# Mixing's first batch in another order: channel weights decoded first, the first group's angles while tokens still load, several token sums at once in separate banks

## The chip, the cores and the metric

The kernel runs on one core of a Trainium2 chip. The metric is device time in microseconds (us). Five engines work beside each other, each through its own instructions in order: PE (matrix products), DVE and ACT (vector work, ACT also sine and absolute value), POOL (more vector work and the indirect transfers), and SP, which here only issues DMA transfers. PE writes into PSUM, which this kernel divides into banks of 128 x 512 float32; SBUF holds everything else.

## The reference

Three stages follow each other; the change is in the third alone.

```python
scores = where(q @ k.T * scale >= max - tau, ..., -1e9); x = softmax(scores) @ v     # attention
out[b, s] = p[e] * (relu(x[b, s] @ w1[e]) @ w2[e])          # one of 8 experts per token
theta = x @ w_theta                                         # mixing, x: (4, 576, 512)
zr, zi = x * cos(theta), x * sin(theta)
y = einsum('ts,bsd->btd', w_tok_r, zr) + einsum('ts,bsd->btd', w_tok_i, zi)
u = x + y
return u + maximum(u @ w_ch, 0)
```

## The kernel before

Attention runs to about 300 us, the routed experts to about 616 us, mixing from there to the end. Every matrix product is made of three: operands are split into a high and a low part (names ending in h and l), and high x high, high x low and low x high are summed in PSUM.

**Weights.** The weights come as 64-bit words. To decode one block of 128 x 512 (`decode_chunk`) takes four DVE instructions (L1109, L1113, L1116, L1118), one square on POOL (L1110), then a copy on ACT and a subtraction on POOL (L1101, L1102, both in `split_last`) that make the high and the low part. `decode(n)` writes n such DVE steps into the order, with two blocks in flight; `decode_rest` writes what is left. The channel weights `ch` are four such blocks, of 0.5 MB of words each (L1075).

**A batch of mixing.** The 576 tokens of a batch are five chunks: four of 128, and one of 64, which two batches share. `prep` transposes a chunk (L1290, PE), takes the high part (xTh, ACT, L1291) and the low part (xTl, DVE, L1292), and copies the sum to xTf (ACT, L1296; the last 64 columns by POOL at L1280). `theta(b, dh, g)` makes the angles of half dh of the channels (256 each) for group g of the chunks (0: chunks 0 and 1; 1: chunks 2 and 3; 2: the fifth), 24 products (L1311 to L1313), 12 for group 2. `wave_steps` takes them on, step by step: k on ACT (L1330), four DVE steps that bring the angle into range (L1332, L1334, L1336, L1338), absolute value, sine and cosine on ACT (L1339 to L1341), two products with x on DVE (L1344, L1346; for the fifth chunk four small ones, L1353), and the split of the results: zrh, zih, zmh on ACT (L1360), zrl, zil, zml on POOL (L1361). A string such as `self.wave("0011")` says which group advances next: each digit is one step of that group.

`mix(b, dh, g)` then sums 27 products (L1374 to L1376) over all z of half dh into one bank, for one quarter g of its outputs: four such sums per half. `mix_out` adds x (u, DVE, L1387) and after two quarters splits u (uu: ACT L1389, DVE L1390). `channel` multiplies u with the channel weights (L1400 to L1402), adds (DVE, L1404), and `store` transposes and writes out.

**Order.** PE, ACT and DVE run their instructions in the order in which the code writes them (`MANUAL`); POOL and the DMA queue of SP are put in order by a scheduler. In batch 0, `prep` handles all five chunks first, then all angles of both halves are multiplied, then the waves run, then the sums `mix`, one bank at a time from a pool of two (`ps_y`). The channel weights are decoded between the sums of batch 0, one block at a time (`decode(4)`). Batch b+1 is prepared between the sums of the second half of batch b.

```python
            self.mix(b, 1, 0)
            self.mix_out(b, 1, 0)
            if more:
                self.prep(b + 1, (0, 1), (0, 1))
```

Of the kernel before, what the change touches and what calls it, by code (L numbers as in the profile page):

```python
# [15 lines left out]
ALU = mybir.AluOpType  # L16
# [19 lines left out]
RING, HIDDEN_STEPS, LAST_STEPS, PRE_STEPS = 3, 4, 5, 9  # L36
# [15 lines left out]
class Kernel:  # L52
# [1080 lines left out]
    def mixing(self):  # L1133
        nc, tc = self.nc, self.tc
        with ExitStack() as ctx:
            def pool(name, bufs, **kw):
                return ctx.enter_context(tc.tile_pool(name=name, bufs=bufs, **kw))
            self.ch = pool("chp", 1).tile([P, 2, 4, DM], F32R, name="ch")
            self.zp, self.xp3, self.tmp = pool("zp", 2), pool("xp3", 1), pool("tmp", 2)
# [3 lines left out]
            self.state3 = [{} for _ in range(B)]  # L1143
            self.work = []
            with tc.manual_schedule(engines=MANUAL):
                self.mix_all(ctx)

    def mix_all(self, ctx):
# [13 lines left out]
        self.prep(0, (3,), (1,))  # L1162
        self.decode(3)
        self.theta(0, 0, 0)
        self.prep(0, (4,), (2,))
        for dh in range(2):
            for g in range(1 - dh, 3):
                self.theta(0, dh, g, self.ps_v if dh or g == 2 else self.ps_th)
        self.waves(0, 0)
        self.wave("0d1")  # L1170
        self.prep(0, (), (3, 4))
        self.wave("0d0d0d0" "21d1d1d1" "00" "0" "2d2d2d2" "11" "1" "22" "2")
# [3 lines left out]
        self.open_stage(1, 2)  # L1176
        self.todo = self.square_words("moe2_w_ch", self.ch)
        self.stage_words()
        self.waves(0, 1)
        self.wave("012" "01010101" "2222")  # L1180
        self.rest = []
        for b in range(B):
            more = b + 1 < B
            self.mix(b, 0, 0)
            while self.rest:
                self.rest.pop(0)()
            self.mix_out(b, 0, 0)
            self.wave("0011" "0")
            self.mix(b, 0, 1)
            self.mix_out(b, 0, 1)  # L1190
            if b == 0:
                self.decode(4)
            self.wave("1")
            self.mix(b, 0, 2)
            self.mix_out(b, 0, 2)
            self.wave("222")
            self.mix(b, 0, 3)
            self.mix_out(b, 0, 3)
            if b == 0:
                self.decode(4)  # L1200
            if more:
                self.load_x(b + 1)
            self.mix(b, 1, 0)
# [3 lines left out]
            self.mix(b, 1, 1)  # L1207
            self.mix_out(b, 1, 1)
            if more:
                chunks = (2, 3) if b % 2 == 0 else (2, 3, 4)  # L1210
                self.prep(b + 1, chunks, chunks)
                if b == 0:
                    self.decode(4)
# [6 lines left out]
            if b == 0:  # L1220
                self.decode_rest()
                self.stage.close()
                self.op = self.right.enter_context(self.tc.tile_pool(name="op", bufs=4, side="right"))
# [23 lines left out]

    def waves(self, b, dh):
        self.work = [self.wave_steps(b, dh, g) for g in range(3)]
# [9 lines left out]
    def load_x(self, b):  # L1259
# [3 lines left out]
        if b % 2:  # L1263
            for n in ("x", "xh", "xl"):
                st[n] = self.state3[b - 1][n]
        else:
            st["x"] = self.xp3.tile([P, NC, DM], F32, name="xm")
        x, m = st["x"], self.m_dram[b * S:]
        for c, e in ((0, 2), (2, 4)) if b else ((0, 1), (1, 2), (2, 4)):
            nc.sync.dma_start(x[:, c:e, :], m[c * P:e * P, :].rearrange("(c p) d -> p c d", p=P))  # L1270
        if b % 2 == 0:
            for t in range(2):
                nc.sync.dma_start(x[t * D:(t + 1) * D, 4, :], m[t * S + 4 * P:(t + 1) * S, :])
            st["xh"] = self.xp3.tile([P, 4, NC * P], F32R, name="xTh")
            st["xl"] = self.xp3.tile([P, 4, NC * P], F32R, name="xTl")
# [6 lines left out]
    def prep(self, b, chunks, rest=()):  # L1282
# [3 lines left out]
        for c in chunks:  # L1286
# [5 lines left out]
            nc.vector.tensor_tensor(st["xl"][:, :, cs], t, st["xh"][:, :, cs].bitcast(F32), ALU.subtract)  # L1292
# [199 lines left out]
```

## Time and profile before

| what | us |
|---|---|
| three runs | 878.38, 882.13, 882.84 (median 882.13) |
| profiled execution | 878.96 |
| its span | 877.1 |
| PE busy in the span | 819.7 (93%) |
| DVE, ACT, POOL busy | 608.8, 480.4, 267.1 |

The profiled execution is 878.96 us by the same clock as the runs; its span, from the first to the last instruction in the trace, is 877.1 us, so 1.9 us lie around it. All times in the trace count from the start of the span. Matrix instructions overlap each other, so their durations are longer than their distance. Idle time before an instruction is printed in square brackets with what ended it.

### The profile page before, as it was taken

The page shows a single profiled execution, that of the slowest core. Times are in us where ns is not written, and L with a number is a line of the kernel's source. Part 1 is how long each engine was busy: PE and PEld are TensorE (multiplying, and loading weights), DVE is VectorE, ACT ScalarE, POOL GpSimd, SP SyncE. Part 2 cuts the span into 40 slices and gives each one's busy share as a digit, 9 for nine tenths or more (in the row PEclk, how much of TensorE's full clock was granted, in tenths as well). Part 3 has the DMA queues.
Part 4 walks back from the last instruction along what each step waited for, and adds up shares of the span by engine and source line. Part 5 has one row for each costly group of instructions (what it writes and reads, how often), then busy time and mean ns, then how long its engine had stood idle before and what let it go on. Part 6 is the DMA issues. An engine that isn't in the chain of part 4 may idle for free.

```text
span 877.1 us, 15357 instructions
## 1 busy us (share of the span) xinstructions
PE 819.7 (93%) x5608; PEld 659.2 (75%) x5608; DVE 608.8 (69%) x1245; ACT 480.4 (55%) x803; POOL 267.1 (30%) x289
## 2 busy tenths in 40 slices
PE   7999998999899995899999999989788999999997
PEld 4565555656556653688999889966688999999997
DVE  6888786887679948539888888545198854745432
ACT  5777675766576654536555556455364533536311
POOL 4222124224114205216445554111125530331220
PEclk9999999999899999999999999999999999999999
DMA  6423213312321269248877787764203020030101
GB/s 164 103 58 99 57 58 92 86 56 69 97 68 59 57 239 235 84 145 275 298 239 257 260 265 240 247 251 138 70 1 96 25 93 23 1 102 1 37 19 54
DMA packets 64903, 105.67 MB, mean 120 GB/s; under 512 B 28338, under 2 KB 32566, under 8 KB 64824
## 3 DMA queue, kind: packets, MB, share of 16 engines
q1 hardware_dynamic: 60632, 94.15, 34.9%
q0 software_dynamic: 4192, 10.51, 3.5%
q8 instruction: 45, 0.74, 0.4%
q14 instruction: 34, 0.28, 0.1%
HBM read 98.67 MB, written 15.40 MB: 130 GB/s over the span
## 4 chain that ended last, share of the span: by engine, by line
PE 32%; DVE 8%; issue 5%; DMA 5%; ACT 2%; POOL 1%; SPq 0%; DVEq 0%; POOLq 0%; ACTq 0%
PE y L1376 3%; PE y L1374 3%; PE y L1375 3%; PE o L951 2%; PE v L1401 2%; PE o L952 2%; PE o L950 2%; PE v L1402 2%; PE v L1400 2%; PE h L935 2%; PE h L934 2%; PE h L933 2%; DMA scr_m<-raw,idx 1%; PE th L1313 1%; PE th L1312 1%
## 5 line engine op out<-in xcount | busy, mean ns | idle before, releaser
L314 ACT ACTIVATE e<-ns,nb 128x576 f32<-128x576 f32 x144 | 111.8, 777 | 59.1 <-DVE ns L308 57.9
L308 DVE TENSOR_SCALAR_CACHE_REDUCE ns<-s,nqs 128x576 f32<-128x576 f32 x144 | 116.7, 811 | 26.0 <-PE s L288 15.9
L346 DVE SCALAR_TENSOR_TENSOR a<-ns,thr,e 128x576 f32<-128x576 f32 x144 | 117.0, 813 | 11.9 <-POOL thr L321 8.3
L321 POOL TENSOR_SCALAR thr<-nb,tauoff 128x2 f32<-128x2 f32 (+1 forms) x80 | 57.0, 713 | 170.3 <-DVE ns L308 170.1
L288 PE MATMUL s<-raw 64*128 64x288 f32 x512 | 87.5, 442 | 15.0 <-DVE ns L308 14.5
L361 ACT ACTIVATE aT<-t 128x512 f32<-128x512 f32 x128 | 70.4, 594 | 28.4 <-PE t L360 27.3
L401 PE MATMUL o<-aT,vm 128*64 128x288 f32 x512 | 78.2, 427 | 0.0
L288 PEld LDWEIGHTS s<-raw 64*128 64x128 f32 x512 | 42.4, 186 | 43.1 <-DVE ns L308 21.2
L933 PE MATMUL h<-xh,stk 128*128 128x256 f32 x256 | 73.3, 286 | 0.0
L1031 DVE TENSOR_TENSOR w2l<-w2r,w2h 128x1024 fp32r<-128x1024 f32 x50 | 64.4, 1296 | 12.2 <-ACT w2h L1030 11.1
L934 PE MATMUL h<-xl,stk 128*128 128x256 f32 x256 | 72.5, 283 | 0.0
L935 PE MATMUL h<-xh,stk 128*128 128x256 f32 x256 | 72.4, 283 | 0.0
L360 PE MATMUL t<-ident,a 128*128 128x128 f32 x512 | 70.6, 279 | 1.5 <-ACT aT L361 1.5
L360 PEld LDWEIGHTS t<-ident,a 128*128 128x128 f32 x512 | 58.0, 143 | 14.6 <-issue 10.5
L401 PEld LDWEIGHTS o<-aT,vm 128*64 128x64 f32 x512 | 32.0, 138 | 38.0 <-issue 25.1
L1030 ACT ACTIVATE w2h<-w2r 128x1024 fp32r<-128x1024 f32 x50 | 52.4, 1060 | 14.4 <-DMA w2r<-in_moe_w_dram 7.8
L1361 POOL TENSOR_TENSOR zrl<-tk,zrh 128x512 fp32r<-128x512 f32 x16 | 23.3, 1459 | 95.4 <-ACT zrh L1360 94.8
L951 PE MATMUL o<-w2l,hh 128*128 128x512 f32 x128 | 50.2, 392 | 0.5 <-DVE w2l L1031 0.4
L950 PE MATMUL o<-w2h,hh 128*128 128x512 f32 x128 | 50.7, 396 | 0.0
L952 PE MATMUL o<-w2h,hl 128*128 128x512 f32 x128 | 50.0, 390 | 0.0
L933 PEld LDWEIGHTS h<-xh,stk 128*128 128x128 f32 x256 | 49.1, 192 | 0.9 <-DVE hl L938 0.3
L934 PEld LDWEIGHTS h<-xl,stk 128*128 128x128 f32 x256 | 49.1, 192 | 0.5 <-issue 0.2
(345 smaller groups left out, 2196.3 us busy)
## 6 DMA issues: line engine op xcount, KB each, us to landing
w2r<-in_moe_w_dram SPq DMA_DIRECT2D x56, 512.0 KB
raw<-in_moe_w_dram SPq DMA_DIRECT2D x42, 512.0 KB
raw<-in_q_dram SPq DMA_DIRECT2D x15, 576.0 KB
w1r<-in_moe_w_dram SPq DMA_DIRECT2D x14, 512.0 KB
raw<-in_k_dram SPq DMA_DIRECT2D x30, 176.0 KB
vm<-in_v_dram SPq DMA_DIRECT2D x32, 128.0 KB
scr_x<-x SPq DMA_DIRECT2D x16, 256.0 KB
out_dram<-ob SPq DMA_DIRECT2D x16, 256.0 KB
```

The costliest lines, as they stand in the source:

```text
L288: nc.tensor.matmul(s[:, z, :SH], qd[rows, int(j != z), cs], kd[rows, j * KH:j * KH + SH], start=True, stop=True)
L308: nc.vector.tensor_scalar(ns, s[:, :, :SH], self.nqs[:, 0:1], None, ALU.mult, ALU.min, accum_out=nb)
L314: self.nc.scalar.activation(e, pr["s", c, j], AF.Exp, bias=pr["nb", c][:, j:j + 1], scale=-1.0)
L346: nc.vector.scalar_tensor_tensor(a.rearrange("p (z s) -> p z s", z=2), s, thr, e, ALU.is_le, ALU.mult, accum_out=total)
L360: nc.tensor.transpose(t[:, i, :], al(c)[:, k * P:(k + 1) * P], self.ident)
L361: nc.scalar.activation(aT[:, 4 * j:4 * j + 4, c * P:(c + 1) * P], t, AF.Copy)
L401: nc.tensor.matmul(o[j * D:(j + 1) * D, :SH], vm[:, j, c - 1, :], aT[:, 4 * j + c - 1, zs], start=(z == 0 and c == 1), stop=(z == 1 and c ...
L933: nc.tensor.matmul(h[:, i], wh[:, fs], xh, start=(k == 0), stop=False)
L934: nc.tensor.matmul(h[:, i], wh[:, fs], xl, start=False, stop=False)
L935: nc.tensor.matmul(h[:, i], wl[:, fs], xh, start=False, stop=(k == 3))
L950: nc.tensor.matmul(o, hh, wh[:, i], start=(q == i == 0), stop=False)
L951: nc.tensor.matmul(o, hh, wl[:, i], start=False, stop=False)
```

## The change

The channel weights are now decoded before anything else of mixing. Their four loads of 0.5 MB are issued together and have four places to land (`open_stage(4, 4)`; before, one place after the first). Then only chunks 0 and 1 are prepared, the angles of the first group of half 0 are multiplied, and its waves run while the other chunks are prepared. The low parts of chunks 2 to 4 (`prep_low`) come after the first four range steps. The products `theta` take another order, and the waves of both halves are written before any u. xTf of batch 0 isn't copied by ACT: POOL adds its high and low part, one instruction of 128 x 1152 for each half (`whole`). zil of half 0 is subtracted by DVE, not by POOL. The sums of half 0 go four at a time, in four banks of two pools (`mix_many`): first the products with zr of all four, then those with zi, then those with zm; the first two sums of half 1 go together in two banks of `ps_v`. POOL's instructions stand in written order too. Chunks 2 and 3 are loaded by two transfers. Later batches keep their order (`first_half` is the code that stood in the loop).

```diff
-            with tc.manual_schedule(engines=MANUAL):
+            with tc.manual_schedule(engines=MANUAL | {mybir.EngineType.Pool}):
                 self.mix_all(ctx)
...
-        self.load_x(0)
-        self.ahead = True
-        while len(self.staged) < RING and self.todo:
-            self.stage_words()
+        self.ahead = True
+        self.stage.close()
+        self.open_stage(4, 4)
+        self.todo = self.square_words("moe2_w_ch", self.ch)
+        for _ in range(4):
+            self.stage_words()
+        self.load_x(0)
         self.warm_up(self.ps_y.tile([P, 512], F32, name="y"), WARM_MIX)
-        self.decode(PRE_STEPS)
-        self.prep(0, (0, 1, 2), (0,))
...
+        self.decode(11)
+        self.prep(0, (0, 1))
         self.theta(0, 0, 0)
-        self.prep(0, (4,), (2,))
...
         self.decode_rest()
...
+        self.work = [self.wave_steps(0, dh, g) for dh in range(2) for g in range(3)]
+        self.wave("0")
+        self.prep(0, (2, 3, 4), low=False)
+        self.wave("0000")
+        self.prep_low(0, (2, 3, 4))
+        self.theta(0, 1, 0, self.ps_v)
+        self.theta(0, 0, 1)
+        self.theta(0, 0, 2, self.ps_v)
+        for g in range(1, 3):
+            self.theta(0, 1, g, self.ps_v)
+        self.wave("000" "111" "0" "11" "2" "333" "111" "3" "1" "3" "2222" "444" "222")
+        self.whole(0, 0)
+        self.mix_many(0, 0, range(4), (self.ps_y, self.ps_y, self.ps_th, self.ps_th))
+        self.wave("44" "333" "55555" "444" "555")
+        for g in range(4):
+            self.mix_out(0, 0, g)
+        self.whole(0, 1)
         self.rest = []
         for b in range(B):
             more = b + 1 < B
-            self.mix(b, 0, 0)
...
+            if b:
+                self.first_half(b)
             if more:
                 self.load_x(b + 1)
-            self.mix(b, 1, 0)
+            if b:
+                self.mix(b, 1, 0)
+            else:
+                self.mix_many(b, 1, range(2), (self.ps_v, self.ps_v))
             self.mix_out(b, 1, 0)
...
+    def whole(self, b, dh):
+        st = self.state3[b]
+        h, l = (st[n][:, 2 * dh:2 * dh + 2, :S].bitcast(F32) for n in ("xh", "xl"))
+        self.nc.gpsimd.tensor_tensor(st["xf", dh], h, l, ALU.add)
...
-            nc.gpsimd.tensor_tensor(zl, z, zh.bitcast(F32), ALU.subtract)
+            if b == dh == 0 and n == "i":
+                yield
+            (nc.vector if b == dh == 0 and n == "i" else nc.gpsimd).tensor_tensor(zl, z, zh.bitcast(F32), ALU.subtract)
...
+    def mix_many(self, b, dh, gs, pools):
+        st = self.state3[b]
+        names = {self.ps_y: "y", self.ps_th: "th", self.ps_v: "v"}
+        for g, pool in zip(gs, pools):
+            st["y", g] = pool.tile([P, 512], F32, name=names[pool])[:, :SH]
+        for steps in (range(4), range(4, 8), range(8, 9)):
+            for g in gs:
+                self.mix_steps(b, dh, g, steps)
```

On DVE, at the start of mixing, the program before goes from the two constants to the low parts of the five chunks and then to the first angle (numbers tell buffers apart; L1332 is the first range step):

```order
L1154 MEMSET round_7323 128x1
L1292 TENSOR_TENSOR xTl_7332<-v_7364,xTh_7331 128x4x128
L1292 TENSOR_TENSOR xTl_7332<-v_7371,xTh_7331 128x4x128
L1292 TENSOR_TENSOR xTl_7332<-v_7378,xTh_7331 128x4x128
L1292 TENSOR_TENSOR xTl_7332<-v_7387,xTh_7331 128x4x128
L1292 TENSOR_TENSOR xTl_7332<-v_7421,xTh_7331 128x4x128
L1332 TENSOR_SCALAR tk2_7531<-tk2_7531 128x512
```

At the same place DVE now has 16 decode steps, of which the last eleven rows up to the first range step (L1359) are these:

```order
L1109 TENSOR_SCALAR val_7393<-w64_7340 128x512
L1109 TENSOR_SCALAR val_7398<-w64_7342 128x512
L1113 SCALAR_TENSOR_TENSOR val_7393<-w64_7340,val_7393 128x512
L1317 TENSOR_TENSOR xTl_7301<-v_7404,xTh_7300 128x4x128
L1317 TENSOR_TENSOR xTl_7301<-v_7411,xTh_7300 128x4x128
L1113 SCALAR_TENSOR_TENSOR val_7398<-w64_7342,val_7398 128x512
L1116 SCALAR_TENSOR_TENSOR val_7393<-w64_7340,val_7393 128x512
L1116 SCALAR_TENSOR_TENSOR val_7398<-w64_7342,val_7398 128x512
L1118 SCALAR_TENSOR_TENSOR val_7393<-ch_7305,val_7393 128x512
L1118 SCALAR_TENSOR_TENSOR val_7398<-ch_7305,val_7398 128x512
L1359 TENSOR_SCALAR tk2_7460<-tk2_7460 128x512
```

Two low parts instead of five stand ahead of the first range step, and the first of them stands behind eleven decode steps.

On POOL, at the same place and through batch 0, the rows are now (a name's digit after zr, zi, zm is its group; xTf of 1152 elements is `whole`):

```order
L1102 TENSOR_TENSOR ch_7305<-val_7393,ch_7305 128x512
L1102 TENSOR_TENSOR ch_7305<-val_7398,ch_7305 128x512
L1391 TENSOR_TENSOR zrl0_7596<-tk2_7460,zrh0_7595 128x512
L1391 TENSOR_TENSOR zrl1_7627<-tk2_7602,zrh1_7626 128x512
L1391 TENSOR_TENSOR zml2_7657<-tr1_7615,zmh2_7656 128x256
L1324 TENSOR_TENSOR xTf_7350<-xTh_7300,xTl_7301 128x1152
L1391 TENSOR_TENSOR zrl0_7781<-tk2_7618,zrh0_7780 128x512
L1391 TENSOR_TENSOR zil0_7785<-tq2_7620,zih0_7784 128x512
L1391 TENSOR_TENSOR zrl1_7802<-tk2_7646,zrh1_7801 128x512
L1391 TENSOR_TENSOR zil1_7806<-tq2_7648,zih1_7805 128x512
L1391 TENSOR_TENSOR zml2_7814<-tr1_7789,zmh2_7813 128x256
L1324 TENSOR_TENSOR xTf_7351<-xTh_7300,xTl_7301 128x1152
```

Two long additions are new among POOL's subtractions; the second stands behind the last subtraction of half 1.

On DVE, at the end of batch 0's waves, the program before has a u between the small products of the fifth chunk and a block of decode ahead of them:

```order
L1118 SCALAR_TENSOR_TENSOR val_7716<-ch_7299,val_7716 128x512
L1387 TENSOR_TENSOR u_7760<-y_7732,xTf_7333 128x288
L1353 TENSOR_TENSOR tr1_7618<-tk1_7617,xm_7325 64x256
L1353 TENSOR_TENSOR tr1_7618<-tq1_7619,xm_7325 64x256
L1353 TENSOR_TENSOR xm_7325<-tk1_7617,xm_7325 64x256
L1353 TENSOR_TENSOR xm_7325<-tq1_7619,xm_7325 64x256
L1387 TENSOR_TENSOR u_7760<-y_7771,xTf_7333 128x288
```

Now the four u of half 0 stand behind all products of half 1:

```order
L1380 TENSOR_TENSOR xm_7299<-tk1_7788,xm_7299 64x256
L1380 TENSOR_TENSOR xm_7299<-tq1_7790,xm_7299 64x256
L1432 TENSOR_TENSOR u_7817<-y_7661,xTf_7350 128x288
L1432 TENSOR_TENSOR u_7817<-y_7662,xTf_7350 128x288
L1435 TENSOR_TENSOR uu_7818<-u_7817,uu_7818 128x576
L1432 TENSOR_TENSOR u_7823<-th_7663,xTf_7350 128x288
L1432 TENSOR_TENSOR u_7823<-th_7664,xTf_7350 128x288
L1435 TENSOR_TENSOR uu_7824<-u_7823,uu_7824 128x576
L1432 TENSOR_TENSOR u_7892<-v_7836,xTf_7351 128x288
```

What moved is every u of half 0 behind the second half's angles, and the decode out from between them.

## Rows read from the trace of the kernel before

**Rows 1.** Windows of mixing, busy us of each engine
```profile
core 0: us, PE busy (x) PEld busy (x) DVE busy (x) ACT busy (x) POOL busy (x), PEclk, DMA share, GB/s
628.00:634.00 6.00, 5.73 (x37) 5.73 (x38) 1.39 (x2) 2.19 (x6) 0.00 (x0) 0.72 0.00 1
634.00:656.00 22.00, 19.27 (x152) 18.46 (x150) 20.02 (x33) 14.09 (x30) 6.73 (x6) 1.00 0.01 1
656.00:676.30 20.30, 16.36 (x125) 16.16 (x125) 18.14 (x26) 8.25 (x18) 10.37 (x8) 1.00 0.30 84
699.00:877.00 178.00, 173.06 (x1351) 172.38 (x1349) 87.74 (x157) 65.58 (x127) 37.46 (x30) 1.00 0.13 41
```

**Rows 2.** PE's own timeline: start, us, engine, line, out<-in, [idle before <-releaser]
```profile
656.62 0.41 PE L1374 MATMUL y<-wt,zrh 128*128 128x288 f32 x1 [2.10 <-DVE u L1387]
667.37 0.37 PE L1374 MATMUL y<-wt,zrh 128*128 128x288 f32 x1 [3.31 <-DVE u L1387]
676.27 0.36 PE L1311 MATMUL th<-th,xTh 128*128 128x256 f32 x1
698.18 0.41 PE L1401 MATMUL v<-uu,ch 128*128 128x320 f32 x1 [0.80 <-DVE uu L1390]
```

**Rows 3.** DVE's timeline, start of mixing and first group
```profile
622.45 0.06 DVE L1152 MEMSET halfpi<- 128x1 f32 x1 [12.57 <-ACT halfpi L1151]
635.91 0.43 DVE L1332 TENSOR_SCALAR tk<-tk 128x512 f32<-128x512 f32 x1 [0.43 <-ACT tk L1330]
640.47 0.68 DVE L1344 TENSOR_TENSOR tk<-tk,xm 128x512 f32<-128x512 f32 x1
641.68 0.28 DVE L1332 TENSOR_SCALAR tk<-tk 128x256 f32<-128x256 f32 x1
642.98 1.42 DVE L1338 TENSOR_SCALAR tr<-tr 128x256 f32<-128x256 f32 x1
```

**Rows 4.** DVE's timeline, decode and second half
```profile
661.23 1.52 DVE L1109 TENSOR_SCALAR val<-w 128x512 int32<-128x512 int32 x1
667.14 0.40 DVE L1353 TENSOR_TENSOR tr<-tk,xm 64x256 f32<-64x256 f32 x1
668.92 0.46 DVE L1387 TENSOR_TENSOR u<-y,xTf 128x288 f32<-128x288 f32 x1
678.75 1.28 DVE L1292 TENSOR_TENSOR xTl<-v,xTh 128x512 fp32r<-128x512 f32 x2
679.95 0.42 DVE L1109 TENSOR_SCALAR val<-w 128x512 int32<-128x512 int32 x1
680.40 0.69 DVE L1113 SCALAR_TENSOR_TENSOR val<-w,val 128x512 int32<-128x512 int32 x1
```

**Rows 5.** POOL's timeline
```profile
642.95 1.30 POOL L1361 TENSOR_TENSOR zrl<-tk,zrh 128x512 fp32r<-128x512 f32 x1 [6.94 <-ACT zrh L1360]
660.65 1.82 POOL L1361 TENSOR_TENSOR zil<-tq,zih 128x512 fp32r<-128x512 f32 x1
668.50 0.98 POOL L1361 TENSOR_TENSOR zml<-tr,zmh 128x256 fp32r<-128x256 f32 x1 [2.92 <-ACT zmh L1360]
678.12 1.61 POOL L1110 TENSOR_TENSOR ch<-w 128x512 fp32r<-128x512 f32 x1 [5.44 <-DMA w<-in_moe_w_ch_dram]
```

**Rows 6.** ACT's timeline, first group
```profile
638.41 0.66 ACT L1339 ACTIVATE tk<-tr 128x512 f32<-128x512 f32 x1
638.93 0.66 ACT L1340 ACTIVATE tq<-tr 128x512 f32<-128x512 f32 x1
640.07 0.50 ACT L1330 ACTIVATE tk<-v,round 128x256 f32<-128x256 f32 x1
640.59 0.63 ACT L1339 ACTIVATE tk<-tr 128x512 f32<-128x512 f32 x1
```

**Rows 7.** Windows in the experts' last part, where the channel weights' loads move
```profile
550.00:555.00 5.00, 5.00 (x44) 5.00 (x43) 3.07 (x4) 3.09 (x4) 0.00 (x0) 1.00 1.00 343
560.00:565.00 5.00, 5.00 (x24) 4.13 (x23) 4.66 (x6) 3.78 (x4) 0.40 (x1) 1.00 0.45 154
```

More of the change, by code (lines that the diff above doesn't have):

```diff
@@ L1137, in pool @@
                 return ctx.enter_context(tc.tile_pool(name=name, bufs=bufs, **kw))
+            self.xp3 = pool("xp3", 1)
+            self.state3 = [{} for _ in range(B)]
+            self.state3[0]["x"] = self.xp3.tile([P, NC, DM], F32, name="xm")
+            for n in "hl":
+                self.state3[0]["x" + n] = self.xp3.tile([P, 4, NC * P], F32R, name="xT" + n)
             self.ch = pool("chp", 1).tile([P, 2, 4, DM], F32R, name="ch")
-            self.zp, self.xp3, self.tmp = pool("zp", 2), pool("xp3", 1), pool("tmp", 2)
+            self.zp, self.tmp = pool("zp", 2), pool("tmp", 2)
             self.ps_y, self.ps_th = pool("ps_y", 2, space=PSUM), pool("ps_th", 2, space=PSUM)
@@ L1219, in mix_all @@
             self.mix_out(b, 1, 2)
[L1220 to L1223, printed above, removed]
             if more:
@@ L1246, in mix_all, with first_half @@
             step()
+    def first_half(self, b):
+        self.mix(b, 0, 0)
+        while self.rest:
+            self.rest.pop(0)()
+        self.mix_out(b, 0, 0)
+        self.wave("0011" "0")
+        self.mix(b, 0, 1)
+        self.mix_out(b, 0, 1)
+        self.wave("1")
+        self.mix(b, 0, 2)
+        self.mix_out(b, 0, 2)
+        self.wave("222")
+        self.mix(b, 0, 3)
+        self.mix_out(b, 0, 3)
     def waves(self, b, dh):
@@ L1273, in load_x @@
                 nc.sync.dma_start(x[t * D:(t + 1) * D, 4, :], m[t * S + 4 * P:(t + 1) * S, :])
-            st["xh"] = self.xp3.tile([P, 4, NC * P], F32R, name="xTh")
-            st["xl"] = self.xp3.tile([P, 4, NC * P], F32R, name="xTl")
+            if b:
+                for n in "hl":
+                    st["x" + n] = self.xp3.tile([P, 4, NC * P], F32R, name="xT" + n)
         for dh in range(2):
@@ L1280, in load_x, with prep @@
                 nc.gpsimd.tensor_tensor(xf[:, :, 4 * P:], h, l, ALU.add)
-    def prep(self, b, chunks, rest=()):
+    def prep(self, b, chunks, rest=(), low=True):
         nc = self.nc
@@ L1365, in mix, with mix_steps @@
     def mix(self, b, dh, g):
+        st = self.state3[b]
+        st["y", g] = y = self.ps_y.tile([P, 512], F32, name="y")[:, :SH]
+        self.mix_steps(b, dh, g, range(9))
+    def mix_many(self, b, dh, gs, pools):
+        st = self.state3[b]
+        names = {self.ps_y: "y", self.ps_th: "th", self.ps_v: "v"}
[4 more added lines that the diff above has]
+                self.mix_steps(b, dh, g, steps)
+    def mix_steps(self, b, dh, g, steps):
         nc = self.nc
@@ L1370, in mix @@
         dd, zs = slice(d * P, (d + 1) * P), slice(z * SH, (z + 1) * SH)
-        st["y"] = y = self.ps_y.tile([P, 512], F32, name="y")[:, :SH]
-        for i, j in enumerate(MIX_ORDER):
-            zh, zl = st["z", dh, j]
+        y = st["y", g]
+        for i in steps:
+            zh, zl = st["z", dh, MIX_ORDER[i]]
             nc.tensor.matmul(y, zh[:, dd], self.wt[:, 0, i, zs], start=(i == 0), stop=False)
```

53 lines of the change are left out of this document (14 added, 39 removed).

## The prediction, made before the changed kernel had run

> **What bounds the kernel now.** I read the windows of the mixing stage first. From 699 us to the end PE is busy 173.06 of 178 us, and its clock is granted in full [rows 1]: whatever comes late at 699 stays late, since there is no idle time in which to make it up. Ahead of that, in the stretch that the change rewrites, PE is busy 19.27 of 22 and 16.36 of 20.3 us, so it idles 2.7 and 3.9 us, 6.6 in all, and DVE is the fuller engine there, 20.02 of 22 and 18.14 of 20.3. PE's timeline says for what it waits: 2.10 and 3.31 us for a u of DVE, since only two banks take sums and the u stands in DVE's order behind angles and decode; 0.80 more for uu at 698.18 [rows 2]. The change can win these, about 7 us, if DVE delivers in time. So DVE's own order in batch 0 is the place to add up.
>
> A second thing in DVE's rows decides the sizes. L1109 takes 0.42 us at 679.95 and 1.52 at 661.23, L1338 on half a tile 1.42 at 642.98 where the same kind of step on that tile, L1332 at 641.68, takes 0.28 [rows 3, 4]. Each long one stands while POOL runs a subtraction: 642.95 for 1.30, 660.65 for 1.82 [rows 5]. Instructions that read one operand from PSUM aren't stretched: u at 668.92 takes 0.46 during the subtraction from 668.50, and two low parts take 1.28 from 678.75 during POOL's square from 678.12 [rows 4, 5]. So in this kernel DVE stands still behind a POOL instruction unless its operand comes from PSUM.
>
> By the Trainium skill ("SBUF — State Buffer", section "Who interferes with whom"), VectorE and GpSimd share a pair of SBUF ports that the one who starts first holds for its whole instruction, while a DVE instruction with at most one SBUF input, outside its two-port modes, isn't held; the rows above agree. The rule speaks against this change, which hands POOL two additions of 1152 elements in the stretch where DVE is the fuller engine; by it the sum below is +5.9 us, and were the port not shared it would be +2.4.
>
> **Start of mixing.** The sum runs on the clock of the trace of before. DVE is free at 622.45 and begins its first angle at 635.91 [rows 3]. Now 16 decode steps stand first: four blocks of 0.42 + 3 x 0.69 = 2.5 us are 10.0 [rows 4], two low parts 1.3, which ends at 633.8. POOL's four squares and first two subtractions run in this time; at half a collision to one each (1.52 - 0.42 = 1.1 for a full one), I put 2 us for them: 635.8. Then ACT copies the last block and makes k, 0.5 + 0.6 [rows 6], and POOL's last two subtractions hold the first range step to about 638.0: 2.1 later than before. The bounds are -1 (no collision, 634.9 with the copy and k) and +4 (all collide in full). The first low part stands behind eleven steps, so the first angle product ends at 636.2 on PE instead of 633.5; nothing on PE but this batch waits behind it.
>
> **DVE from 638.0 to the last product of half 1.** What DVE has to do of its own: four groups of four range steps at 2.28 (635.91 to 640.47 holds two groups, rows 3), 9.1; two half-size ones at 1.45, 2.9; three low parts 1.9; eight products at 0.6, 4.8; two times four small products at 1.78 (667.14 to 668.92, rows 4), 3.6; two zil 1.2. Sum 23.5.
>
> What it waits for ACT: the string of waves lets one group follow the next without a spare one between, so DVE stands each time that k is queued behind other ACT work. One absolute value, sine, cosine and k(half size) are 2.18 us (638.41 to 640.59, rows 6). I count a wait of 1.1 for k of group 1, which stands behind zrh and zih of group 0; 2.8 for that run of four with one more k of 0.6; 1.9 and 2.1 for k of the two groups of half 1. Sum 7.9. Before, the decode steps and the u's lay in such gaps; they are gone from there.
>
> What it waits for POOL: 2.0 behind the first half's zrl; 2.5 behind the first whole addition; 0.5 and 1.3 behind the second half's subtractions. Sum 6.3. No row shows an addition of 128 x 1152. A subtraction of 512 takes 1.30 and one of 256 takes 0.98 [rows 5]; along the line through these two it is 2.1 us, in proportion to 512 it is 2.9. I take 2.6, nearer to the proportion, since a row of 512 in the same place runs to 1.82; 2.1 and 2.9 stay as bounds.
>
> The Trainium skill ("SBUF — State Buffer", section "SBUF: two separate sides") gives GpSimd's port about 614 GB/s; two operands of 1152 would pass one read port in an estimated 1.9 us. No run here shows that width; a subtraction of 512 would by the same reckoning be 0.85 where the row shows 1.30, so I go by the row. By the page's figure the sum would be 0.7 lower for each of the two additions that is waited for.
>
> So the last product of half 1 ends at 638.0 + 23.5 + 7.9 + 6.3 = 675.7. In the trace of before the last small product ends at 668.9, with the first u's and 1.5 blocks of decode done by then.
>
> **PE.** A matrix instruction costs 173.06 / 1351 = 0.128 us [rows 1]. From 636.2: transposes 1.3, 96 angle products 12.3, 108 products of half 0's four sums 13.8, so these end at 663.4 without a wait. This is the gain that the change is after: before, the last of the four sums began at 667.37 + 3.5. But no u can start: all four stand behind 675.7 on DVE. PE then has only the first sums of half 1, 54 products, 6.9 us, and these need z's whose subtraction POOL ends at 675.3 and 676.4. So PE's last product of them is at about 678.2, after some 8 us of idle time, which takes the place of the 5.4 in rows 2.
>
> **Behind it.** POOL's second whole addition comes after the last subtraction, 676.4 to 679.1, and DVE's uu (both operands in SBUF) stands behind it; the u of half 1 needs it as well. Then uu, two u, uu, u, low parts, u: 679.7, 680.3, 681.8, 682.1, 683.5. The transposes of chunks 2 and 3 of batch 1 need the banks that the last two of these free, and the angle products of batch 1, which stand behind them on PE, begin at 684.4. Before they began at 676.27 [rows 2]: +8.1. From there PE has 162 products ahead of the end of the first channel products that need the last uu, 20.2 us (0.125 each, more than half of them being the shorter angle and channel products), to 704.6. Before, that point lay 0.6 behind 698.18 [rows 2], at 698.75, and 698.75 - 676.27 = 22.5: 2.3 us of idle time lay between, the 0.80 of rows 2 among them. Now no decode stands ahead of the u's that PE waited for there, so I count the 2.3 as saved. 704.6 - 698.75 = +5.9.
>
> **What costs nothing.** ACT loses ten copies of xTf (some 3 us of its 14.09 in 22), which isn't on the path. The four loads of channel weights, 2.1 MB, move among the experts' loads: the queues are full at 550 to 555 and at 0.45 at 560 to 565 [rows 7]; 2.1 MB at 343 GB/s are 6.1 us, of which one load was there before. The loads behind them on SP's queue are the experts' second weights; they are used 9 us and more later, so I put 0, and +1 as the other end, below zero nothing since transfers are only added. The split load of chunks 2 and 3 and the written order of POOL: 0, within 0.3 either way, since the first use of those chunks is behind the decode. Where batch 0 is done, the order of the later batches is as before.
>
> **The sum.** +5.9 with every collision at its price, +2.4 with none. I take +5.0, nearer to the upper end as most rows that could collide do. On the profiled execution, 878.96, this is 884.0. The runs' median is 882.13, 3.2 above it; on the median it is 887.1, and that is the forecast.
>
> **Rivals.**
> 1. *The sums run on without a stop.* If half 1's z's are ready when half 0's sums end at 663.4, angle products of batch 1 begin at about 672 and the 2.3 us ahead of the channels are gone: -6, 876. For it: PE's own work allows it, and DVE is relieved of 10 us of decode in the middle. Against it: of DVE's 14.2 us of waiting (7.9 + 6.3) 12 would have to vanish; it decides at a last product near 664, and it turns into no loss when 6 of them do. Chance 0.18.
> 2. *POOL's long additions fall where DVE waits anyway*, or pass beside DVE's PSUM operands. Then 2.5 and 2.7 us go from the sum, with a little of the rest: +1.6, 883.7, no difference. For it: DVE waits 7.9 us for ACT in the same stretch. Against it: the first stands right behind zml, when DVE has range steps to do. Chance 0.30.
> 3. *The experts' weights come late as well.* If the queue at 550 to 565 passes its spare share, the experts end 1 to 3 us later on top: 889 to 890. For it: rows 7 show it full at 550; against it, the uses are late. Chance 0.10, part of the slower cases.
>
> The forecast itself has 0.42. A measurement of this kernel can tell about 0.5%, 4.4 us, from no change. Faster than that is rival 1: 0.18. Within it are rival 2 and a few of the smaller forms of the forecast: 0.31. Slower is the rest, 0.51. The range: below, 2.4 to 8.3 is what the sum spans as its terms go to their bounds, so 884 to 891 is the likeliest case's own range; to leave no more than 2 in 10 out it reaches down to 876.5 for most of rival 1, and up to 892.
>
> **What the profile after would show.** The first range step at about 638; decode rows at its front of 1.2 us and more; no PE idle time inside half 0's sums; an idle PE of some 7 to 8 us between 663 and 678; the second whole addition at 676 with uu behind it; angle products of batch 1 at 684, where before it was 676.3; from then on the same PE density. I am wrong if half 1's products are done on DVE by 666, if the whole additions leave DVE's rows short, or if PE's clock falls in the idle time, which it didn't after the 3.31 us in rows 2.

## The result, and the profile after

The changed kernel takes 887.12 us in the median of ten runs, that of before, on the same chip in the same session, 881.73. The ratio is 1.0071, 95% interval 1.0043 to 1.01: slower, by 6 us in round figures. On another chip, with the experiments, it was 1.0062 (1.0039 to 1.0084); both intervals lie wholly above 1.

The profiled execution is a long one of its kind, 893.12 us with a span of 891.4, so its first rows have to be read with care. SP issues the first token load of mixing 6.8 us later than in the profile of before; these are SP's rows of both, before and then after:

```profile
621.00 1.31 SPq L1270 DMA_DIRECT2D xm<-scr_m  x3
```

```profile
627.79 1.99 SPq L1282 DMA_DIRECT2D xm<-scr_m  x4
```

What comes behind this point is the stage that was rewritten, so all distances from here on count from the first token load. From there to the end it is 877.1 - 621.00 = 256.1 us before and 891.4 - 627.79 = 263.6 after: +7.5 in this pair of profiles. The 6.8 us ahead of it are taken up with the experiments.

The first group's angle products begin 636.09 - 627.79 = 8.3 us behind the first token load. Before it was 629.89 - 621.00 = 8.9, since the kernel before, too, multiplies these 24 products ahead of the fifth chunk's transposes, and not behind all five chunks; on PE little is gained there. On DVE the decode stands ahead of the first range step, and POOL's subtractions stand beside it:

```profile
629.13 2.10 DVE L1109 TENSOR_SCALAR val<-w 128x512 int32<-128x512 int32 x2 [0.18 <-DVE round L1159]
634.77 0.75 DVE L1109 TENSOR_SCALAR val<-w 128x512 int32<-128x512 int32 x2
637.24 1.58 DVE L1113 SCALAR_TENSOR_TENSOR val<-w,val 128x512 int32<-128x512 int32 x1
638.74 2.38 DVE L1116 SCALAR_TENSOR_TENSOR val<-w,val 128x512 int32<-128x512 int32 x2
641.04 1.28 DVE L1118 SCALAR_TENSOR_TENSOR val<-ch,val 128x512 f32<-128x512 f32 x2
642.47 2.73 POOL L1102 TENSOR_TENSOR ch<-val,ch 128x512 fp32r<-128x512 f32 x2 [2.49 <-ACT ch L1101]
```

DVE's timeline of the changed kernel shows the prediction's chain. The columns are start, duration, engine, line, operation, and in brackets the idle time and who ended it:

```profile
643.60 0.44 DVE L1359 TENSOR_SCALAR tk<-tk 128x512 f32<-128x512 f32 x1 [1.27 <-ACT tk L1357]
650.61 0.45 DVE L1359 TENSOR_SCALAR tk<-tk 128x512 f32<-128x512 f32 x1 [1.27 <-ACT tk L1357]
656.28 0.43 DVE L1359 TENSOR_SCALAR tk<-tk 128x512 f32<-128x512 f32 x1 [2.77 <-ACT tk L1357]
659.33 1.61 DVE L1391 TENSOR_TENSOR zil<-tq,zih 128x512 fp32r<-128x512 f32 x1
664.69 0.43 DVE L1359 TENSOR_SCALAR tk<-tk 128x512 f32<-128x512 f32 x1 [1.90 <-ACT tk L1357]
667.60 1.13 DVE L1363 SCALAR_TENSOR_TENSOR tr<-tk,tr 128x512 f32<-128x512 f32 x1
668.76 2.75 DVE L1365 TENSOR_SCALAR tr<-tr 128x512 f32<-128x512 f32 x1
674.73 0.58 DVE L1359 TENSOR_SCALAR tk<-tk 128x256 f32<-128x256 f32 x1 [2.02 <-ACT tk L1357]
679.13 1.40 DVE L1380 TENSOR_TENSOR xm<-tk,xm 64x256 f32<-64x256 f32 x1
680.57 1.39 DVE L1380 TENSOR_TENSOR xm<-tq,xm 64x256 f32<-64x256 f32 x1
681.99 0.82 DVE L1432 TENSOR_TENSOR u<-y,xTf 128x288 f32<-128x288 f32 x2
683.56 2.25 DVE L1435 TENSOR_TENSOR uu<-u,uu 128x576 fp32r<-128x576 f32 x1 [0.75 <-ACT uu L1434]
```

Behind the first range step, four waits for k are 1.27 + 2.77 + 1.90 + 2.02 = 8.0 us. The long rows, 1.61, 1.13, 2.75, 1.40, 1.39 and 2.25 for work of 0.68, 0.69, 0.43, 0.42, 0.42 and 0.76, stand beside these rows of POOL, the two of 128 x 1152 above all:

```profile
658.77 1.61 POOL L1391 TENSOR_TENSOR zrl<-tk,zrh 128x512 fp32r<-128x512 f32 x1 [8.00 <-ACT zrh L1387]
667.20 0.97 POOL L1391 TENSOR_TENSOR zml<-tr,zmh 128x256 fp32r<-128x256 f32 x1 [6.81 <-ACT zmh L1387]
668.14 3.08 POOL L1324 TENSOR_TENSOR xTf<-xTh,xTl 128x1152 f32<-128x1152 f32 x1
678.82 1.43 POOL L1391 TENSOR_TENSOR zrl<-tk,zrh 128x512 fp32r<-128x512 f32 x1 [2.37 <-ACT zrh L1387]
680.21 1.47 POOL L1391 TENSOR_TENSOR zil<-tq,zih 128x512 fp32r<-128x512 f32 x1
682.52 2.68 POOL L1324 TENSOR_TENSOR xTf<-xTh,xTl 128x1152 f32<-128x1152 f32 x1
```

PE has no wait inside half 0's four sums any more, where before it had 2.10 and 3.31 [rows 2]. Its wait now stands ahead of half 1:

```profile
673.87 0.61 PE L1419 MATMUL v<-wt,zrh 128*128 128x288 f32 x1 [4.06 <-ACT zrh L1387]
688.48 0.66 PE L1303 MATMUL v<-ident,xm 128*128 128x128 f32 x4 [2.70 <-DVE u L1432]
690.49 0.56 PE L1338 MATMUL th<-th,xTh 128*128 128x256 f32 x1
```

The second row is a second wait, for a u, ahead of batch 1's transposes. The third is batch 1's first angle product: 62.7 us behind the first token load, against 676.27 - 621.00 = 55.3 before [rows 2]. Windows of this stretch, with the column PEclk (the granted clock, 1.00 is 2.4 GHz, 0.50 is 1.2 GHz) behind the five engines:

```profile
634.80:640.80 6.00, 4.71 (x21) 4.53 (x22) 6.00 (x9) 1.68 (x4) 4.99 (x3) 0.50 0.00 0
669.80:673.80 4.00, 0.02 (x1) 0.00 (x0) 2.91 (x3) 2.26 (x5) 1.42 (x1) 0.87 0.00 0
673.80:679.40 5.60, 5.02 (x19) 4.68 (x20) 4.42 (x9) 3.20 (x9) 3.13 (x3) 0.50 0.31 95
690.40:693.20 2.80, 2.80 (x16) 2.80 (x15) 1.96 (x3) 2.35 (x7) 0.00 (x0) 0.50 0.00 0
705.80:883.80 178.00, 177.62 (x1381) 177.18 (x1380) 88.52 (x159) 66.94 (x130) 40.74 (x32) 1.00 0.11 34
```

The clock is at its lower level in three of these windows: for batch 0's first angle products, after the 4.06 us without products, and for batch 1's first angle products, after 2.70 and 0.63 us of idle time with four transposes between. The first costs nothing: those products end at 641.8, and ACT, which copies the last decoded blocks until 643.0, makes k at 642.90. The last window lies where the fourth of [rows 1] does, moved by 6.8. It ends 7.6 us ahead of the end of the span, that of before at the end, where PE runs out of work. From the first add behind a channel product to 7.6 us ahead of the end, PE is busy 170.3 of 170.7 us before and 171.1 of 171.5 now: equally full, so nothing is made up, and 0.7 us more are lost there.

### The profile page after: what moved, and what is told of

Its sections match the earlier page's. It is cut to its first block, busy times and chain, and to the rows that moved or that the text cites. A ratio compares the mean times of both kernels' runs of the same rounds, so it can differ in the third digit from the quotient of the medians.

```text
span 891.4 us, 15330 instructions
## 1 busy us (share of the span) xinstructions
PE 829.8 (93%) x5608; PEld 668.1 (75%) x5608; DVE 609.0 (68%) x1247; ACT 478.4 (54%) x793; POOL 266.0 (30%) x289
## 4 chain that ended last, share of the span: by engine, by line
PE 42%; DVE 7%; DMA 7%; issue 5%; ACT 2%; POOL 1%; SPq 0%; DVEq 0%; POOLq 0%; ACTq 0%
PE y L1419 3%; PE y L1420 3%; PE y L1421 3%; DMA scr_m<-raw,idx 3%; PE h L934 3%; PE h L935 3%; PE h L933 3%; DMA xt<-scr_x,idx 2%; PE o L951 2%; PE o L952 2%; PE o L950 2%; PE v L1446 2%; PE v L1447 2%; PE v L1445 2%; PE th L1340 1%
## 5 line engine op out<-in xcount | busy, mean ns | idle before, releaser
L314 ACT ACTIVATE e<-ns,nb 128x576 f32<-128x576 f32 x144 | 111.8, 776 | 58.9 <-DVE ns L308 56.2
L1031 DVE TENSOR_TENSOR stk<-raw,stk 128x1024 fp32r<-128x1024 f32 x36 | 44.3, 1251 | 8.7 <-ACT stk L1030 8.5
```

The lines of the kernel that those rows point to most:

```text
L314: self.nc.scalar.activation(e, pr["s", c, j], AF.Exp, bias=pr["nb", c][:, j:j + 1], scale=-1.0)
L1031: nc.vector.tensor_tensor(lo, raw, hi.bitcast(F32), ALU.subtract)
```

## The experiments

Each ran beside the kernel before on the same chip and in the same session, on four chips in all; the changed kernel again and the three single edits that follow it share one. "Angle product" is the distance from the first token load to batch 1's first angle product, "first add" that to the first DVE add behind a channel product, "stage" that to the end of the span, each of one profile in us; the ratio is of the times to those of before, with its interval.

| kernel | angle product | first add | stage | ratio |
|---|---|---|---|---|
| before, first profile | 55.3 | 77.8 | 256.1 | |
| before, again | 56.0 | 77.9 | 256.2 | 1.0011 (0.9988 to 1.0035) |
| changed, first profile | 62.7 | 84.6 | 263.6 | 1.0071 (1.0043 to 1.01) |
| changed, again | 62.8 | 84.0 | 263.0 | 1.0062 (1.0039 to 1.0084) |
| additions on DVE | 58.9 | 80.7 | 259.7 | 1.0034 (1.0015 to 1.0053) |
| decode spread | 60.1 | 82.3 | 261.4 | 1.0041 (1.0017 to 1.0065) |
| k ahead | 60.0 | 81.6 | 260.7 | 1.0032 (1.0011 to 1.0054) |
| filler on PE | 62.8 | 84.0 | 263.1 | 1.0077 (1.0055 to 1.0099) |
| the three edits | 57.1 | 77.6 | 256.7 | 1.0029 (1.0003 to 1.0055) |
| with early u | 55.3 | 78.3 | 257.3 | 1.0007 (0.9984 to 1.0029) |
| with a late fourth block | 54.1 | 77.0 | 256.1 | 1.0001 (0.9972 to 1.0029) |
| before, four banks | 57.5 | 79.3 | 257.7 | 0.9996 (0.9971 to 1.002) |
| channel loads late | 69.2 | 90.9 | 269.9 | 1.0158 (1.0124 to 1.0192) |

**The changed kernel again.** No edit.

> The changed kernel once more, for a second profile of it. The first profile is 14.3 us longer than that of before, of which the mixing stage (from its first token load to the end) holds 7.5 and the part ahead of it 6.8. My theory: only the mixing part belongs to the change, so this run is 4 to 8 us over before, its mixing stage again 262 to 265 us against 256.1, and its first token load moves back towards 621 to 625. Rival, the early loads of the channel weights delay the experts: the first token load stays at 627 or later.

The stage is 263.0 and repeats; the first token load comes at 627.96 and doesn't move back, as the rival had it. The kernel before was profiled once more too:

> The kernel before once more, for a profile on the same chip as the experiments. My theory (the part ahead of mixing is the same in both, and only drifts from chip to chip and execution to execution): the mixing stage from its first token load to the end is 256 us within 1, against 263.0 to 263.6 of the changed kernel, and the first token load may come anywhere from 621 to 628. Rival (the early loads of channel weights delay the experts): the first token load comes 3 us or more ahead of the changed kernel's on the same chip, that is at or below 624.5.

Its stage is 256.2, so 6.8 to 7.5 us of difference belong to mixing, which is all of the ratio's 5.5 to 6.3 and a little more. Its first token load is at 622.49, where the rival wanted it; but that execution, 880.57 us, is far below its median of 887.14. Worked out from medians instead (median time less stage less the 1.9 us around the span), the part ahead of mixing is 885.6 - 256.2 - 1.9 = 627.5 before and 891.57 - 263.0 - 1.9 = 626.7 changed: no delay that the spread of the runs would show.

**The loads among the experts' loads.** Two kernels issue channel loads from ACT's queue at the start of mixing. The edit is that of the second, without the lines that set `ch_late`.

```diff
-                self.nc.sync.dma_start(w[dst], s)
+                (self.nc.scalar if self.ch_late else self.nc.sync).dma_start(w[dst], s)
```

> The changed kernel with its four loads of channel weights issued by ACT at the start of mixing, so that none of them lies among the experts' loads. Decode starts later, so the mixing stage grows by 2 to 5 us. What tells is the part ahead of mixing, as median time less the mixing stage of the profile less 1.9. My theory (the early loads cost the experts nothing): it is 626 to 629, as in the changed kernel and before. Rival (they delay the experts): 624.5 or less.

This one sent the loads of every mixing weight from ACT's queue, not those of the channel weights alone; the experts became slower (905.79 - 271.4 - 1.9 = 632.5 us ahead of mixing), the ratio was 1.023, and it tells nothing on the question. The second has the edit as meant:

> As the kernel with late loads, but only the four loads of channel weights are issued by ACT at the start of mixing; the earlier one moved the loads of all mixing weights to ACT's queue. What tells is the distance from SP's last load of a token list to the first token load: 44.1 to 45.1 in three profiles with one channel load among the experts' loads, 45.2 to 47.8 in seven with four. Theory (the early loads cost the experts nothing, and these differ by chance): 45.2 to 47.8 stays likely. Rival (they cost about 1.4 us): 44.0 to 45.1. The mixing stage grows by 2 to 8 us in either case, since decode waits for the loads.

The distance is 626.47 - 581.30 = 45.2 us, on the border between the two. The border itself is less sharp than that: eight profiles have four early loads, with the additions on DVE at 628.82 - 583.71 = 45.1, so they span 45.1 to 47.8, with a mean of 45.9, against 44.1 to 45.1, mean 44.5. Between SP's last two loads of token lists, where the channel loads are issued, 32.7 us pass with them and without (580.00 - 547.31 in the changed kernel, 576.73 - 544.04 before). From medians the part ahead of mixing is 899.35 - 269.9 - 1.9 = 627.5, again as before. So a cost of the early loads isn't seen above 1.5 us, and one below that stays open. That decode must not wait for its words shows well: the stage grows by 6.3.

**Additions on DVE.**

```diff
-        self.wave("000" "111" "0" "11" "2" "333" "111" "3" "1" "3" "2222" "444" "222")
+        self.wave("000" "111" "0" "11" "2" "3")
         self.whole(0, 0)
+        self.wave("33" "111" "3" "1" "3" "2222" "4")
+        self.whole(0, 1)
+        self.wave("44" "222")
...
-        self.whole(0, 1)
...
-        self.nc.gpsimd.tensor_tensor(st["xf", dh], h, l, ALU.add)
+        self.nc.vector.tensor_tensor(st["xf", dh], h, l, ALU.add)
```

> Both additions of 128 x 1152 are done by DVE, each at a place where DVE waits for ACT's k, in place of POOL. My theory (POOL's additions hold DVE): the 2.75 us row of the last range step falls to 0.43, the first uu from 2.25 to 0.76, so batch 1's angle products start 3.5 to 4.5 us earlier against the first token load, and the time is 3 to 4.5 us below the changed kernel. Rival (the additions lie beside other waits): within 1 us of the changed kernel.

DVE's timeline has the addition at 1.35 us, half of POOL's 2.68, and the range step and the uu that had stood behind POOL at their own length:

```profile
654.46 1.35 DVE L1326 TENSOR_TENSOR xTf<-xTh,xTl 128x1152 f32<-128x1152 f32 x1
669.78 0.43 DVE L1367 TENSOR_SCALAR tr<-tr 128x512 f32<-128x512 f32 x1
682.26 0.76 DVE L1437 TENSOR_TENSOR uu<-u,uu 128x576 fp32r<-128x576 f32 x1 [0.75 <-ACT uu L1436]
```

The angle product comes 3.9 us earlier and the ratio falls by 0.0028, 2.5 us; by the medians of the two (891.57 and 889.70) it is 1.9. The theory holds in the profile; the time gives back less than the 3 us expected, and more than the rival's 1. POOL's additions are on the path.

**Decode spread.**

```diff
-        self.decode(11)
+        self.decode(5)
...
-        self.decode_rest()
+        self.decode(4)
...
+        self.wave("000" "1" "dd" "11" "0" "11" "2" "3" "dddd" "33" "111" "3" "1" "3" "2222" "4" "d" "44" "222")
```

> The decode of the channel weights is spread: five steps ahead of the first low parts, four behind them while PE multiplies the first angles, the rest in the waits for k and ahead of the additions. Nothing else differs. My theory: the first range step comes 4 to 5 us earlier against the first token load (15.8 us in the changed kernel), and of that 2 to 4 us arrive at batch 1's first angle product, so the time is 2 to 4 us below the changed kernel. Rival (decoding first costs nothing, since PE waits for DVE's second half anyway and the same work comes back there): within 1 us.

```profile
638.07 0.43 DVE L1359 TENSOR_SCALAR tk<-tk 128x512 f32<-128x512 f32 x1 [2.46 <-ACT tk L1357]
667.86 3.11 DVE L1373 TENSOR_TENSOR tq<-tq,xm 128x512 f32<-128x512 f32 x1
```

The first range step comes 11.1 us behind the first token load and not 15.8: 4.8 earlier, as expected. At the angle product 2.6 of it are left, of the time 1.9 by the ratio and 1.4 by the medians, just short of the 2 expected: the spread decode's POOL subtractions and the first long addition stand in the second half, as the row of 3.11 for a product of 0.68 shows.

**k ahead.**

```diff
-        self.wave("000" "111" "0" "11" "2" "333" "111" "3" "1" "3" "2222" "444" "222")
+        self.wave("00" "1" "0" "11" "0" "3" "11" "2" "333" "11" "3" "1" "1" "4" "2222" "44" "22" "5" "2")
...
-        self.wave("44" "333" "55555" "444" "555")
+        self.wave("44" "33" "55" "3" "55" "444" "555")
```

> In batch 0 each group's k is written on ACT ahead of the previous group's split or absolute value, sine and cosine, and the range steps of two groups are interleaved. My theory: DVE's waits for k in the changed kernel (1.3, 2.8, 1.9 and 2.0 us) fall to 2 to 3 in all, and the time is 3 to 5 us below the changed kernel. Rival (the k wait isn't the bound, ACT's sines are, so the waits move to the products): the waits for ACT stay at 6 us or more under another line, and the time is within 1.5 us.

```profile
657.38 1.35 DVE L1391 TENSOR_TENSOR zil<-tq,zih 128x512 fp32r<-128x512 f32 x1 [2.87 <-ACT zih L1387]
664.70 3.15 DVE L1371 TENSOR_TENSOR tk<-tk,xm 128x512 f32<-128x512 f32 x1
```

Only one wait for k is left inside the waves, 1.17 us, but 2.87 come back as a wait for zih, and a product stands 3.15 us at the first long addition. Half went: 4.0 us of waiting for ACT are left, and the angle product comes 2.7 us earlier. Theory and rival each hold for a part; the time, lower by 2.7 us by the ratio and 2.3 by the medians, stays just short of the theory's 3.

**Filler on PE.** The 34 products show as 68 rows and take 7.75 us, more than the idle time they were to fill.

```diff
+            if dh and not g:
+                self.warm_up(t, 34)
```

> The changed kernel with 34 products of ones put on PE ahead of the sums of half 1, in the idle time of 4.1 us; they add no result. My theory: the granted clock stays at 1.00 there, yet the sums of half 1 end no earlier, since they wait for POOL's last subtractions, and the time is that of the changed kernel within 1 us. Rival (the halved clock after the idle time costs what it shows, about 2.5 us): 2 to 3 us below the changed kernel.

```profile
667.72 7.75 PE L240 MATMUL v<-one 128*128 128x128 f32 x68
675.23 0.38 PE L1422 MATMUL v<-wt,zrh 128*128 128x288 f32 x1
688.61 0.56 PE L1338 MATMUL th<-th,xTh 128*128 128x256 f32 x1
```

Half 1's sums now begin 675.23 - 625.82 = 49.4 us behind the first token load, 3.3 later than in the changed kernel (673.87 - 627.79 = 46.1), at a granted clock of 1.00 throughout. PE's wait for a u ahead of batch 1's transposes is 2.67 us as against 2.70, the angle product is at the same 62.8, and the time, at 1.0077, isn't lower. So neither the idle 4.06 us nor the lower clock behind it is what sets the end: DVE's and POOL's chain is. The rival is refuted.

**Together.**

> The three edits together: additions on DVE, decode spread over DVE's waits, k ahead. Alone each took the distance from the first token load to batch 1's first angle product down by 3.9, 2.6 and 2.7 us from 62.7; that of before is 55.3. My theory (three separate waits in one chain on DVE): they add up in the main, the distance is 54 to 56 us and the time within 2 us of before, 6 us below the changed kernel. Rival (each fills the same idle time of DVE, so the second has nothing left to fill): the distance stays at 58 or more and the time 2.5 us or more over before.

```profile
670.42 0.61 PE L1420 MATMUL v<-wt,zrh 128*128 128x288 f32 x1 [6.18 <-ACT zrh L1388]
```

Of 3.9 + 2.6 + 2.7 = 9.2 us singly, 5.7 come together: 57.1, between theory and rival. The stage is 256.7, that of before within 0.6, yet the time is 1.0029, with an interval down to 1.0003; where the other 2 us lie isn't settled. PE's wait has grown to 6.18. From 656.7 us to the last product at 678.2 DVE has no gap left to fill, yet it isn't at its own speed. These are subtractions of POOL and rows of DVE that stand beside them:

```profile
663.85 3.92 POOL L1102 TENSOR_TENSOR ch<-val,ch 128x512 fp32r<-128x512 f32 x2 [1.29 <-ACT ch L1101]
664.89 1.75 DVE L1364 SCALAR_TENSOR_TENSOR tr<-tk,tr 128x512 f32<-128x512 f32 x1
671.67 1.33 POOL L1392 TENSOR_TENSOR zil<-tq,zih 128x512 fp32r<-128x512 f32 x1
671.78 1.77 DVE L1372 TENSOR_TENSOR tk<-tk,xm 128x512 f32<-128x512 f32 x1
674.29 1.33 POOL L1392 TENSOR_TENSOR zrl<-tk,zrh 128x512 fp32r<-128x512 f32 x1 [1.29 <-ACT zrh L1388]
674.49 1.41 DVE L1381 TENSOR_TENSOR tr<-tq,xm 64x256 f32<-64x256 f32 x1
```

From 661 to 678 us such rows are longer than the same steps where POOL is idle by some 7 us in all. No run took all of that out.

**Early u.** On top, the u of half 0 between the last products of half 1, and batch 1's first angle products ahead of its second pair of transposes:

```diff
+        self.wave("44" "33" "55" "3")
+        self.mix_out(0, 0, 0)
+        self.mix_out(0, 0, 1)
+        self.wave("55" "44" "4")
...
+                if b == 0:
+                    self.theta(b + 1, 0, 0)
```

> The three edits, and the u of half 0 written between the last products of half 1, not behind them, and batch 1's first angle products ahead of the transposes of its chunks 2 and 3. My theory (behind half 1's last product stand 4.6 us of u and uu in a row, 1.5 of it waiting for ACT): 1.5 to 3 us below the three edits alone, so 0 to 3 us below before. Rival (DVE's work ahead of the last product grows by what is taken from behind it): within 1 us of the three edits.

The ratio is lower by 0.0022, 2 us (1.3 by the medians), but the two intervals overlap; the angle product stands where it stood before the change. The stage, 257.3, is 0.6 longer than that of the three edits: what is won at the angle product is lost by the first add. By the stage the rival holds, and the 2 us aren't shown to come from this edit.

**A late fourth block.** On top again, three blocks early and one loaded and decoded behind batch 1's preparation.

```diff
-        self.open_stage(4, 4)
-        self.todo = self.square_words("moe2_w_ch", self.ch)
-        for _ in range(4):
+        self.open_stage(3, 3)
+        self.todo = self.square_words("moe2_w_ch", self.ch)[:3]
+        for _ in range(3):
...
+        self.open_stage(1, 1)
+        self.todo = self.square_words("moe2_w_ch", self.ch)[3:]
```

> The version with the early u, but the fourth block of channel weights is loaded and decoded later, behind batch 1's preparation, where DVE waits for PE and ACT; the third is decoded ahead of the second half. My theory (DVE is the bound up to the last product of half 1, and 3 decode steps with two POOL subtractions stand in it): PE's wait of 6.2 us ahead of half 1's sums falls to 2 to 4, the mixing stage is 2 to 4 us below that of the version with the early u (257.3), and the time 1 to 3 us below before. Rival (the fourth block comes back as a wait ahead of the channels): within 1 us of the version with the early u.

```profile
666.70 0.61 PE L1433 MATMUL v<-wt,zrh 128*128 128x288 f32 x1 [2.72 <-ACT zrh L1401]
```

PE's wait, 6.18 with the three edits, is 2.72, as expected. The stage falls by 1.2 and not by 2 to 4; the time is 1.0001 of before and not 1 to 3 us below it, which is the rival's size. It is the best version of the change, and it isn't faster than the kernel before.

**The banks alone**, in the kernel before:

```diff
-        st["y"] = y = self.ps_y.tile([P, 512], F32, name="y")[:, :SH]
+        y = (self.ps_th.tile([P, 512], F32, name="th") if b == dh == 0 and g > 1
+             else self.ps_y.tile([P, 512], F32, name="y"))
+        st["y"] = y = y[:, :SH]
```

> The kernel before with one edit: the third and fourth sum of batch 0's first half use the two banks of the angle products' pool, so that none of the four waits for a bank. Nothing else of the change. My theory (DVE's chain sets the start of batch 1, not the banks): PE's waits for u in the sums, 5.4 us, go, but come back ahead of the first sum of half 1, which needs z's that end at 664 to 669; batch 1's first angle product moves by less than 1.5 us and the time is within 0.2% of before. Rival (the banks were the bound): 3 us or more below before.

```profile
674.31 0.61 PE L1376 MATMUL y<-wt,zmh 128*128 128x288 f32 x1 [2.04 <-ACT zmh L1360]
682.87 0.36 PE L1311 MATMUL th<-th,xTh 128*128 128x256 f32 x1
```

The waits of 2.10 and 3.31 are gone, and 2.04 plus some shorter ones have come in half 1. The angle product is 57.5 behind the first token load, 1.6 to 2.2 later and not within 1.5; the first range step is as much later in that profile already (16.3 against 14.9 and 14.1). From the first range step to the angle product it is 41.2 us, between the 40.4 and 41.9 of the two profiles of before. The time is that of before. The banks weren't the bound.

## Why the prediction was right

The forecast was slower, 887.1 us, and the time is 887.12; the difference to before was put at +5.0 and is +5.4 (6 by the ratio, between 3.8 and 8.8 by its interval). The direction and the chain of waits are what was right. That the figure is met to the hundredth is luck: the stage itself grew by 6.8 to 7.5 us, and +5.0 was a choice between the sum's +5.9 and its +2.4. The +2.4 doesn't follow from the terms: without the 3.1 us at the start and the 6.3 behind POOL the last product of half 1 would stand at 666.3, 9.4 earlier, while rival 2, which takes out 2.5 and 2.7, comes to +0.7 by its own terms and not to +1.6. Times of the changed kernel are moved back here by 6.8 to the clock of before.

- *Start.* The first range step was put at 638.0 and stands at 643.60 - 6.79 = 636.8: +0.9, not +2.1. The decode ended where I had it, at 641.04 + 1.28 - 6.79 = 635.5 (put at 635.8). Its collisions were dearer than the 2 us taken: three of its 16 steps are long, by some 3.3 us together. The others put at 0.69 took 0.64 where two of a kind follow each other. What was too dear is the 1.1 us for POOL's last two subtractions: they run from 642.47 to 645.20, and the first range step beside them, 0.44 us, has its own length.
- *DVE's waits for ACT*, 7.9, are 8.0. Taking k ahead shows that they are on the path, but not in full.
- *DVE's waits for POOL*, 6.3: the long rows above hold 1.0 + 0.4 + 2.3 + 1.0 + 1.0 = 5.7 up to the last product, and some 0.9 lie in smaller ones. The first long addition, put at 2.6 with bounds of 2.1 and 2.9, took 3.08, outside; the second took 2.68. The rows at 512 set the proportion well; the line through 256 and 512 was the wrong end. The estimate of 1.9 that I worked out from a figure of the Trainium skill ("SBUF — State Buffer", section "SBUF: two separate sides") is refuted by both rows. The Trainium skill prices the same thing elsewhere, at about 2.6 cycles of GpSimd for an element of a two-operand addition ("GPSIMD Engine Reference", section "3.1 Elementwise — side-by-side cycle accounting"), an estimate of 2.5 us, near the row's 2.68.
- *The last product of half 1* was put at 675.7 and ends at 681.96 - 6.79 = 675.2.
- *PE.* Half 0's sums end at 663.0 by the same shift (put at 663.4, though its terms add up to 663.6) without a wait. The idle time ahead of the end of half 1's first sums was put at 8 us; it is 4.06 and 0.8 in short ones, since the sums begin when the first z of half 1 is there and then run at half the clock; another 2.70 and 0.63 follow ahead of batch 1's angle products. A fall of the clock was named as a sign of being wrong, and it fell. It costs nothing behind the 4.06 us, as the filler shows, and about 1.1 us at batch 1's first twelve angle products, which start 0.21 us apart, not 0.12, and stand on the path. The second profile of the changed kernel has a mean of 0.72 over the same 2.8 us and the filler's 0.77, and both have their first add 0.5 us earlier.
- *Batch 1's first angle product*: put at 684.4, stands at 683.7: +7.4, where I had +8.1.
- *Channels.* I counted 2.3 us of idle time as saved ahead of them. The first add is at 712.34 - 6.79 = 705.6, +6.8 to before: 0.7 were saved, the clock took part of the rest. The term was too generous by 1.6; that the start was too dear by 1.2 made up for most of it, and that two errors cancel is luck as well.
- *The rivals.* That the sums run on without a stop was refuted by the 4.06 us. That POOL's additions lie beside other waits was refuted by putting them on DVE, where 3.9 us went at the angle product. That the experts' weights come late can't be seen above 1.5 us.

So the price is one of order: the sums of half 0 lost their waits, but every u was put behind DVE's work for half 1, with the decode ahead of it and POOL's long additions in it, and batch 1 starts from the u's. The banks alone change nothing, and with all three costs taken out again the stage is that of before within 0.6 us, the time 1.0029 of it. Not tried by themselves were the subtraction of zil on DVE, POOL's written order and the split token load.

## What to carry to other kernels

A wait that PE loses is worth something only if the engine that it waited for has room: here DVE carried the path into batch 1, and PE's 5.4 us came back as 4.06 and 2.70 in other places. Before a decode or an addition is moved to the front or to POOL, ask on which engine the chain to the next batch runs, and whether the moved instruction shares anything with it. Savings of edits that fill the same engine's gaps need not add up (here 9.2 us singly, 5.7 together).

## What the runs showed of the hardware

- An addition of 128 x 1152 float32 takes 1.35 us on DVE and 2.68 to 3.08 on POOL, and on POOL it holds DVE's instruction for up to 2.3 us as well.
- The granted clock behind an idle time isn't the same in each execution. In the first profile of before PE stood 3.31 us and went on at 1.00; in the second it stood 3.33, and these are the windows of the idle time and of what followed:

```profile
664.60:668.00 3.40, 0.09 (x1) 0.01 (x1) 3.33 (x5) 0.00 (x0) 1.63 (x1) 1.00 0.06 10
668.00:673.00 5.00, 4.98 (x26) 5.00 (x27) 4.14 (x7) 1.62 (x3) 3.85 (x4) 0.66 0.31 98
```

- The part ahead of mixing drifts by some 8 us between executions of nearly the same code (first token loads from 621.00 to 628.82 in the profiles; 621.00 and 622.49 in those of before, 625.34 with the four banks), while the mixing stage of one kernel repeats within 0.6. A stage is better compared by its own length than by the end of the span.
